# A rewritten exponential chain on VectorE, ten probability slots, five query sets

## The chip, the cores and the metric

The kernel runs on one core of a Trainium2 chip. The metric is the device time of one execution in microseconds (us); the median of five executions of the kernel before is 1861.48 us (1855.05 to 1868.85). The engines are TensorE (PE in the profile, with its weight loads as PEld), VectorE (DVE), ScalarE (ACT), GpSimd (POOL) and SyncE (SP). Each works through its own queue in order, and they wait for each other on semaphores.

## What is computed

Two layers, each an attention part and a mixer part, on 2048 positions of 512 features. Attention has 32 heads of 16 features that share one set of keys and values. Cut to what matters:

```
def _A_ref(x, wq, wk, wv, wo):               # H = 32, Dh = 16
    q = (x @ wq).reshape(B, S, H, Dh).transpose(0, 2, 1, 3)
    k = x @ wk
    v = x @ wv
    scores = einsum('bhqd,bkd->bhqk', q, k) * Dh ** (-0.5)
    p = softmax(scores, axis=-1)
    o = einsum('bhqk,bkd->bhqd', p, v)
    return o.transpose(0, 2, 1, 3).reshape(B, S, H * Dh) @ wo

def _B_ref(x, w_in, w_sp, b_sp, w_out):      # Fh = 896
    z = gelu(x @ w_in)
    z1, z2 = z[..., :Fh], layernorm(z[..., Fh:])
    g = einsum('ts,bsf->btf', w_sp, z2) + b_sp[None, :, None]
    return (z1 * g) @ w_out

x = x + _A_ref(layernorm(x), ...)
x = x + _B_ref(layernorm(x), ...)            # and both once more
```

The largest elementwise work is the exponential of the scores: 2 layers x 32 heads x 2048 x 2048 of them.

## The kernel before

**Blocks and units.** A group is a set of queries that fill 512 columns, for four partition groups of 32 (four heads at a time); 32 groups make a layer. For each of the 16 key tiles of 128, a group has one unit, and a unit has four blocks of 128 keys x 512 columns: 1024 units and 4096 blocks in all. For each block TensorE makes scores into PSUM (`_qk`, L1697), one engine turns them into probabilities in SBUF, and TensorE multiplies them with the values and adds up over the group's 16 units (PVStream, L1447). The value matrix has a column of ones, so the softmax denominator comes out with the sums, and the maximum is not subtracted. After a group VectorE evacuates (L815), the result is transposed and divided (L827, L839).

**Two engines for the exponential.** ScalarE takes scores from two rings of three and of two PSUM banks (FillStream, ExpStream, L1371) and writes to fifteen slots of `Pa`. VectorE takes single blocks from the remaining banks (DexStream) and writes to eight slots of `Pd`. It works on batches of two blocks: one instruction per block (L1554) turns the score into an integer, 65536 times the base-two logarithm of the result plus the exponent's bias; the low sixteen bits are then the fraction and the high ones the exponent. Six instructions over the whole batch follow (`chain`): u = fraction scaled to 0..1 (L1582), w = u - 1 (L1584), q = u w (L1588), u = B u + A (L1585), q = q u (L1591), and last the integer is scaled down, q is added, and the sum is written as a 16-bit integer whose bits are the bf16 probability (L1593).

**Order of the work.** A planner (`Sched`, at build time) simulates the engines with a list of costs (`d_sb`, `d_psum`, `d_act`) and delays (`LAT`) and commits operations greedily by readiness and priority; each engine's instructions are then written out in that order, with semaphore waits where an operation depends on another. Which block goes to which engine is decided there, too. When TensorE's next fill is committed, `DexStream.take` may give VectorE one block of a later unit, at least `LOOK` units ahead of the fill; it does so only if a bank is free, VectorE's backlog is under `BACKLOG`, fewer than two batches are open, and the slots of `Pd` that the batch will use have been read by their matmuls. It takes no block of the last `ENDX` units of a layer. `SoloStream` does the same between fills. VectorE has other work that the planner mixes in: query casts (L802), evacuations, layer norms and the mixer's sums (L1126, L1127).

**Query sets.** The queries of a group are projected into one of `NQS` sets in `qs` (`make_q`). `start_q` makes the first `NQS` of them; when the last score of a group has been made, `q_released` lets its set be made again for the group `NQS` further on.

**Shared scratch.** The tile `E` holds the chain's intermediates during attention, and the mixer's output weights and products at the end of a layer. [...]

Of the kernel before, what the change touches and what calls it, by code (L numbers as in the profile page):

```python
# [20 lines left out]
NF = 7  # L21
LN_EPS = 1e-5
SCALE = DH ** -0.5
# [338 lines left out]
    return progs  # L362


C_LOG2 = SCALE * 1.4426950408889634 * 65536.0
C_BIAS = 127.0 * 65536.0
C_A = 128.0 * 0.30449799
C_B = 128.0 * 0.07822817

LOOK = 6  # L370
NEAR = 4
URGENT = 1.0
BACKLOG = 3.0
# [1 line left out]
ENDX = 6  # L375
PR_LAST = 0.3
PR_SMALL = 0.6
NQS = 6
NPA = 15
NPD = 8  # L380
NWS = 16


# [4 lines left out]
def d_sb(n, rate):  # L388
    return n * rate + 0.066
# [10 lines left out]
def d_mm(n):  # L400
    return max(n / 2400.0 + 0.006, min(0.045 + n * 0.43e-3, 0.155))
# [19 lines left out]
class Kern:  # L421
    def __init__(self, nc, A_x, A_wq, A_wk, A_wv, A_wo, B_x, B_w_in, B_w_sp, B_b_sp, B_w_out, out):
# [15 lines left out]
        sc = self.sc = Sched([5, 7])  # L438
        self.nsb = 0
        sb = self.sb  # L440
# [295 lines left out]
    def layer_groups(self, layer):  # L736
        t0 = 0
        for ci, n in enumerate(self.chunks):
            nh = 512 // n
            for hg in range(0, 8, nh):  # L740
# [5 lines left out]
                q.index = g.index  # L746
                q.slot = q.index % NQS
                self.qsets.append(q)
# [34 lines left out]
    def make_q(self, q, war=()):  # L783
# [678 lines left out]
class DexStream:  # L1462
# [7 lines left out]
    def __init__(self, k):  # L1470
        self.k = k
        self.u = 0
        self.batch = []
        self.nb = 0
        self.cur = []
        self.open = []
        self.owner = [None] * NPD
        self.end = [None, None]
        self.last = []
        self.gate = None  # L1480

# [8 lines left out]
    def take(self, t, js):  # L1490

        k = self.k
        sc = k.sc
        if sc.bank_free() > t:
            return None
        base = 2 * (self.nb % (NPD // 2))
        if any(o.start is None and o.ready is not None and o.ready <= t for o in k.early_first):
            return None
        want = sum(o.first and o.prio < URGENT and o.ready <= t for o in sc.ready["pe"])
        if want and sum(not b.busy and not b.closed and b.free_at <= t for b in sc.banks) <= want:  # L1500
            return None
        if not self.batch:
            self.open = [o for o in self.open if o.start is None or o.end > t]
            if len(self.open) >= 2:
                return None
            backlog = sc.free["dve"] - t + sum(o.dur for o in sc.ready["dve"] if o.eng == "dve" and o.ready <= t)
            if backlog > BACKLOG:
                return None
            for i in range(2):
                w = self.owner[base + i]  # L1510
                if w is not None and w.pv is None:
                    return None
        fu = k.fill_s.u
        while fu < len(k.units) and all(b.kind is not None for b in k.units[fu].blocks):
            fu += 1
        if fu >= len(k.units):
            return None
        layer = k.units[fu].grp.layer
        u = max(self.u, fu + LOOK)
        while u < len(k.units):  # L1520
            un = k.units[u]
# [12 lines left out]
            u += 1  # L1534
        if u >= len(k.units):
            return None
        x = c[-1]
        x.kind = "D"
        self.u = u + 1
        if not self.batch:  # L1540
            self.ops = []
            self.s = self.nb % 2
            self.base = base
            self.war = [w.pv for w in self.owner[base:base + 2] if w is not None]
            self.nb += 1
        self.owner[self.base + len(self.batch)] = x.unit
        self.batch.append(x)
        return x

    def first_op(self, x, o, j):  # L1550
        k = self.k
        s = self.s
        i = len(self.batch) - 1
        c = k.sc.op("dve", lambda e: e.tensor_scalar(k.eI[:, s, 512 * i:512 * (i + 1)],  # L1554
                                                     k.b32(j.bank.idx)[:, 0:512], C_LOG2, C_BIAS, op0=ALU.mult, op1=ALU.add),
                    d_psum(512), [o, self.end[s]] + (self.gate or []), 2.0, job=j)
        c.unit = x.unit.index
        return c

    def after(self, c):  # L1560
        self.ops.append(c)
        if len(self.batch) == 2:
            self.flush()

    def flush(self):
# [4 lines left out]
    def chain(self, s):  # L1570
        k = self.k
        sc = k.sc
        nb = len(self.cur)
        n = 512 * nb
        I, u, w, q = k.eI[:, s, 0:n], k.eu[:, s, 0:n], k.ew[:, 0, 0:n], k.eq[:, s, 0:n]
        lo = I.bitcast(U16).rearrange("p (n two) -> p n two", two=2)[:, :, 0]
        base = self.base
        pr = 2.8

        def ts(out, a, m, b):  # L1580
            if b is None:
                return lambda e: e.tensor_scalar(out, a, m, None, op0=ALU.mult)  # L1582
            if m is None:
                return lambda e: e.tensor_scalar(out, a, b, None, op0=ALU.add)  # L1584
            return lambda e: e.tensor_scalar(out, a, m, b, op0=ALU.mult, op1=ALU.add)  # L1585
        o2 = sc.op("dve", ts(u, lo, 2.0 ** -16, None), d_sb(n, 0.521e-3), self.ops, pr)
        o3 = sc.op("dve", ts(w, u, None, -1.0), d_sb(n, 0.26e-3), [o2, getattr(self, "wfree", None)], pr)
        o4 = sc.op("dve", lambda e: e.tensor_tensor(q, u, w, ALU.mult), d_sb(n, 0.521e-3), [o3], pr)  # L1588
        self.wfree = o4
        o5 = sc.op("dve", ts(u, u, C_B, C_A), d_sb(n, 0.26e-3), [o4], pr)  # L1590
        o6 = sc.op("dve", lambda e: e.tensor_tensor(q, q, u, ALU.mult), d_sb(n, 0.521e-3), [o5], pr)  # L1591
        po = k.Pd[:, base:base + nb, :].rearrange("p k q -> p (k q)")
        o7 = sc.op("dve", lambda e: e.scalar_tensor_tensor(po.bitcast(U16), I, 2.0 ** -9, q, op0=ALU.mult, op1=ALU.add),  # L1593
                   d_sb(n, 1.042e-3), [o6] + self.war, pr)
        self.end[s] = o7
        for o in (o2, o3, o4, o5, o6, o7):
# [153 lines left out]
```

## Time and profile before

| | |
|---|---|
| median of five executions | 1861.48 us |
| the profiled execution's own time | 1867.65 us |
| its span | 1865.8 us |
| TensorE / VectorE / ScalarE busy | 1592.6 / 1736.4 / 1752.0 us |
| blocks turned into probabilities by ScalarE / VectorE | 3596 / 500 |
| VectorE batches | 251 |
| ScalarE's exp instructions | 1439 |
| mean granted TensorE clock | 0.98 |

A group line of the profile reads: source line, engine, operation, output <- inputs with their shapes, count; then busy time and mean duration in nanoseconds; then the idle time of the engine just before these instructions and what ended it. Rows of stretches give for each engine the busy time and, in brackets, the number of instructions. Durations on one engine can overlap, so a sum of durations may exceed the busy time.

### The profile page before, as it was taken

What the parts mean: (1) busy time and instruction counts of PE and PEld (TensorE: products, weight loads), DVE (VectorE), ACT (ScalarE), POOL (GpSimd) and SP (SyncE); (2) the same over time, 40 slices, a digit from 0 to 9 for tenths busy, and PEclk for the clock granted to TensorE, in tenths of its full rate; (3) what the DMA queues carried; (4) which work ended last, traced back from release to release, by engine and by line L of the source; (5) the groups of instructions that cost most, each with busy time, mean ns of one, the idle gap of its engine ahead of it and who ended that gap; (6) DMA issues with size and microseconds to landing.
All of it is one profiled execution on the core that took longest, in us unless ns stands there. A gap on an engine that the chain in (4) does not pass through costs nothing.

```text
span 1865.8 us, 30131 instructions
## 1 busy us (share of the span) xinstructions
PE 1592.6 (85%) x11779; PEld 475.5 (25%) x11868; DVE 1736.4 (93%) x3108; ACT 1752.0 (94%) x1577; POOL 48.0 (3%) x90
## 2 busy tenths in 40 slices
PE   8877888878889998898887878887788798989989
PEld 3222222112222222222431222221222222322334
DVE  8999999999989899987889999999999999999878
ACT  8999999999989999999569999999999999999983
POOL 2000000000000000000010000000000000000000
PEclk9999999899979999999999999999999999999999
DMA  9800001000010020111120000100000101011123
GB/s 261 208 1 1 10 9 30 1 1 18 7 40 23 24 46 21 46 57 55 48 52 1 1 1 10 37 1 1 1 15 10 40 24 32 15 43 35 60 63 110
DMA packets 122965, 68.04 MB, mean 36 GB/s; under 512 B 76996, under 2 KB 119240, under 8 KB 122824
## 3 DMA queue, kind: packets, MB, share of 16 engines
q1 hardware_dynamic: 121240, 65.95, 13.2%
q8 instruction: 94, 1.54, 0.3%
q14 instruction: 47, 0.39, 0.1%
q10 hardware_dynamic: 1584, 0.16, 0.1%
HBM read 30.97 MB, written 17.83 MB: 26 GB/s over the span
## 4 chain that ended last, share of the span: by engine, by line
ACT 40%; PE 22%; DVE 21%; issue 16%; DMA 1%; POOL 0%; SPq 0%; ACTq 0%; POOLq 0%; DVEq 0%
ACT Pa L1371 38%; PE ps_all L1697 6%; PE ps_all L1113 5%; PE ps_all L1447 4%; DVE E L1554 3%; DVE Pd L1593 3%; PE ps_all L1679 2%; DVE E L1588 2%; DVE E L1591 2%; DVE E L1582 2%; PE ps_all L936 1%; DVE st L631 1%; PE ps_all L1205 1%; DVE E L1585 1%; DVE E L1584 1%
## 5 line engine op out<-in xcount | busy, mean ns | idle before, releaser
L1371 ACT ACTIVATE Pa<-ps_all 128x1536 bf16<-128x1536 f32 (+1 forms) x1439 | 1636.8, 1365 | 31.5 <-PE ps_all L1697 29.4
L1697 PE MATMUL ps_all<-qs,kT 32*128 32x512 bf16 x4096 | 572.7, 390 | 194.4 <-ACT Pa L1371 176.9
L1554 DVE TENSOR_SCALAR E<-ps_all 128x512 int32<-128x512 f32 x500 | 341.2, 685 | 37.0 <-PE ps_all L1697 34.9
L1697 PEld LDWEIGHTS ps_all<-qs,kT 32*128 32x128 bf16 x4096 | 140.3, 91 | 750.0 <-ACT Pa L1371 688.1
L1447 PE MATMUL ps_all<-Pa,V 128*32 128x512 bf16 x3596 | 327.0, 391 | 0.0
L1593 DVE SCALAR_TENSOR_TENSOR Pd<-E 128x1024 uint16<-128x1024 int32 (+1 forms) x251 | 304.5, 1213 | 0.7
L1679 PE MATMUL ps_all<-zero 128*128 128x512 bf16 x780 | 260.6, 405 | 26.6 <-DVE E L1584 3.8
L1113 PE MATMUL ps_all<-wsT,z2n 128*128 128x512 bf16 x650 | 192.2, 391 | 13.3 <-issue 4.3
L1447 PE MATMUL ps_all<-Pd,V 128*32 128x512 bf16 x500 | 178.2, 392 | 0.0
L1588 DVE TENSOR_TENSOR E<-E 128x1024 f16<-128x1024 f16 (+1 forms) x251 | 171.6, 684 | 3.2
L1591 DVE TENSOR_TENSOR E<-E 128x1024 f16<-128x1024 f16 (+1 forms) x251 | 171.5, 683 | 2.4
L1582 DVE TENSOR_SCALAR E<-E 128x1024 f16<-128x1024 uint16 (+1 forms) x251 | 171.7, 684 | 1.6
L1585 DVE TENSOR_SCALAR E<-E 128x1024 f16<-128x1024 f16 (+1 forms) x251 | 105.1, 419 | 2.5
L1584 DVE TENSOR_SCALAR E<-E 128x1024 f16<-128x1024 f16 (+1 forms) x251 | 104.9, 418 | 2.4
L1679 PEld LDWEIGHTS ps_all<-zero 128*128 128x128 bf16 x780 | 61.1, 99 | 167.4 <-issue 91.6
L1447 PEld LDWEIGHTS ps_all<-Pa,V 128*32 128x32 bf16 x3596 | 64.7, 94 | 122.8 <-issue 116.7
L1126 DVE TENSOR_TENSOR gp<-ps_all,gp 128x512 f16<-128x512 f32 x112 | 75.3, 684 | 19.0 <-PE ps_all L1113 18.1
L1113 PEld LDWEIGHTS ps_all<-wsT,z2n 128*128 128x128 bf16 x714 | 54.5, 98 | 108.0 <-issue 64.7
L793 PE MATMUL ps_all<-xnTA,wq_pad 128*128 128x512 bf16 (+2 forms) x384 | 70.6, 310 | 1.3 <-DVE qs L802 0.7
L972 PE MATMUL ps_all<-xnTB,w_in_r 128*128 128x512 bf16 (+2 forms) x336 | 62.8, 311 | 4.0 <-DVE z1s L983 1.4
L936 PE MATMUL ps_all<-w_in_r,xnTB 128*128 128x448 bf16 x256 | 63.2, 356 | 1.3 <-DVE z2n L947 0.6
L1205 PE MATMUL ps_all<-E 128*128 128x512 bf16 x215 | 52.4, 380 | 4.7 <-DVE E L1190 1.8
(90 smaller groups left out, 1009.0 us busy)
## 6 DMA issues: line engine op xcount, KB each, us to landing
wsT_scratch<-gp SPq DMA_DIRECT2D x16, 512.0 KB, 3.9
wsT<-wsT_scratch SPq DMA_DIRECT2D x8, 1024.0 KB, 5.4
z1s<-z_scratch SPq DMA_DIRECT2D x16, 448.0 KB, 3.9
wsT<-wsT_scratch SPq DMA_DIRECT2D x8, 512.0 KB, 3.7
z_scratch<-z1s SPq DMA_DIRECT2D x4, 896.0 KB, 5.6
X<-in_A_x_dram SPq DMA_DIRECT2D x8, 256.0 KB, 5.3
out_dram<-X SPq DMA_DIRECT2D x16, 128.0 KB, 1.8
w_in_r<-in_B_w_in_dram SPq DMA_DIRECT2D x1, 1792.0 KB, 10.2
```

What stands on the lines that cost most here:

```text
L1113: ins = e.matmul(self.b32(b), self.z2n[:, s, f * 128:(f + 1) * 128], w_[:, s - s0, :] if s - s0 < na or not spare else wsp[:, s - s0 - na, :],
L1371: return e.activation(k.Pa[:, base:base + n, :], k.b32(b0, n).rearrange("p (k q) -> p k q", k=n), ACTF.Exp, scale=SCALE)
L1447: ins = e.matmul(k.b32(k.pvb)[32 * j:32 * j + 32, :], k.V[:, u.kt, 32 * j:32 * j + 32], b.slot, tile_position=(0, 32 * j), start=u.first, ...
L1554: c = k.sc.op("dve", lambda e: e.tensor_scalar(k.eI[:, s, 512 * i:512 * (i + 1)], k.b32(j.bank.idx)[:, 0:512], C_LOG2, C_BIAS, op0=ALU.mul ...
L1582: return lambda e: e.tensor_scalar(out, a, m, None, op0=ALU.mult)
L1584: return lambda e: e.tensor_scalar(out, a, b, None, op0=ALU.add)
L1585: return lambda e: e.tensor_scalar(out, a, m, b, op0=ALU.mult, op1=ALU.add)
L1588: o4 = sc.op("dve", lambda e: e.tensor_tensor(q, u, w, ALU.mult), d_sb(n, 0.521e-3), [o3], pr)
L1591: o6 = sc.op("dve", lambda e: e.tensor_tensor(q, q, u, ALU.mult), d_sb(n, 0.521e-3), [o5], pr)
L1593: o7 = sc.op("dve", lambda e: e.scalar_tensor_tensor(po.bitcast(U16), I, 2.0 ** -9, q, op0=ALU.mult, op1=ALU.add), d_sb(n, 1.042e-3), [o6] ...
L1679: return e.matmul(k.b32(k.pvb if b is None else b.idx), k.zero[:], k.zero[:, None, :].to_broadcast([P, 4, P]), start=b is not None, stop=b ...
L1697: return e.matmul(self.b32(bank), self.kT[32 * j:32 * j + 32, kt * 128:(kt + 1) * 128], self.qs[32 * j:32 * j + 32, g.q.slot, :], tile_pos ...
```

## The change

The score is no longer turned into an integer. L1554's successor writes fp32: 128 times the base-two logarithm plus 24576, a value in a range where the low sixteen bits of the fp32 mantissa are the fraction of the logarithm. From that fraction one instruction makes x, shifted and scaled (a multiply and an add). Then w = x x, w = w + C, w = w x, which is a cubic without its square term and so needs five instructions over the batch in place of six. The last instruction adds a constant and w to the fp32 score and writes 16 bits. The kinds of instruction, in order, are: scalar with two operations, product, scalar with one operation, product, closing.

The intermediates x and w have two buffers each (`NXW`); before, u and q had two and w one. `Pd` has ten slots in place of eight, VectorE's look-ahead is eight units in place of six, and there are five query sets in place of six. The batch is still two blocks (`NDB`). `E` becomes smaller.

```
-C_LOG2 = SCALE * 1.4426950408889634 * 65536.0
-C_BIAS = 127.0 * 65536.0
-C_A = 128.0 * 0.30449799
-C_B = 128.0 * 0.07822817
-
-LOOK = 6
+E_LOG2 = SCALE * 1.4426950408889634 * 128.0
+E_BIAS = 24576.0
+E_X = (128.0 * 0.07802455204644283) ** (1.0 / 3.0)
+E_A = 0.9657950762942451
+E_C = -6.696623932488385 * E_X * E_X
+E_D = 127.0 * 128.0 - E_BIAS + 128.0 * 0.43426538197757353
+NDB = 2
+NXW = 2
+
+LOOK = 8
...
-NQS = 6
+NQS = 5
 NPA = 15
-NPD = 8
+NPD = 10
...
-        E = sb([P, 9216], BF16, "E")
-        self.eI = E[:, 0:4096].bitcast(I32).rearrange("p (s n) -> p s n", s=2)
-        self.eu = E[:, 4096:6144].bitcast(FP16).rearrange("p (s n) -> p s n", s=2)
-        self.ew = E[:, 6144:7168].bitcast(FP16).rearrange("p (s n) -> p s n", s=1)
-        self.eq = E[:, 7168:9216].bitcast(FP16).rearrange("p (s n) -> p s n", s=2)
+        nb = 512 * NDB
+        E = sb([P, max((4 + 2 * NXW) * nb, NF * (D + 640))], BF16, "E")
+        self.ey = E[:, 0:4 * nb].bitcast(FP32).rearrange("p (s n) -> p s n", s=2)
+        xw = E[:, 4 * nb:(4 + 2 * NXW) * nb].bitcast(FP16).rearrange("p (two s n) -> p two s n", two=2, s=NXW)
+        self.ex, self.ew = xw[:, 0, :, :], xw[:, 1, :, :]
...
-        c = k.sc.op("dve", lambda e: e.tensor_scalar(k.eI[:, s, 512 * i:512 * (i + 1)],
-                                                     k.b32(j.bank.idx)[:, 0:512], C_LOG2, C_BIAS, op0=ALU.mult, op1=ALU.add),
+        c = k.sc.op("dve", lambda e: e.tensor_scalar(k.ey[:, s, 512 * i:512 * (i + 1)],
+                                                     k.b32(j.bank.idx)[:, 0:512], E_LOG2, E_BIAS, op0=ALU.mult, op1=ALU.add),
                     d_psum(512), [o, self.end[s]] + (self.gate or []), 2.0, job=j)
...
-        o2 = sc.op("dve", ts(u, lo, 2.0 ** -16, None), d_sb(n, 0.521e-3), self.ops, pr)
-        o3 = sc.op("dve", ts(w, u, None, -1.0), d_sb(n, 0.26e-3), [o2, getattr(self, "wfree", None)], pr)
-        o4 = sc.op("dve", lambda e: e.tensor_tensor(q, u, w, ALU.mult), d_sb(n, 0.521e-3), [o3], pr)
-        self.wfree = o4
-        o5 = sc.op("dve", ts(u, u, C_B, C_A), d_sb(n, 0.26e-3), [o4], pr)
-        o6 = sc.op("dve", lambda e: e.tensor_tensor(q, q, u, ALU.mult), d_sb(n, 0.521e-3), [o5], pr)
+        o2 = sc.op("dve", lambda e: e.tensor_scalar(x, lo, E_X * 2.0 ** -16, E_X * E_A, op0=ALU.mult, op1=ALU.add),
+                   d_sb(n, 0.521e-3), self.ops + [self.xfree[s % NXW]], pr)
+        o3 = sc.op("dve", lambda e: e.tensor_tensor(w, x, x, ALU.mult), d_sb(n, 0.521e-3), [o2, self.wfree[s % NXW]], pr)
+        o4 = sc.op("dve", lambda e: e.tensor_scalar(w, w, E_C, None, op0=ALU.add), d_sb(n, 0.26e-3), [o3], pr)
+        o5 = sc.op("dve", lambda e: e.tensor_tensor(w, w, x, ALU.mult), d_sb(n, 0.521e-3), [o4], pr)
         po = k.Pd[:, base:base + nb, :].rearrange("p k q -> p (k q)")
-        o7 = sc.op("dve", lambda e: e.scalar_tensor_tensor(po.bitcast(U16), I, 2.0 ** -9, q, op0=ALU.mult, op1=ALU.add),
-                   d_sb(n, 1.042e-3), [o6] + self.war, pr)
+        o7 = sc.op("dve", lambda e: e.scalar_tensor_tensor(po.bitcast(U16), y, E_D, w, op0=ALU.add, op1=ALU.add),
+                   d_sb(n, 1.042e-3), [o5] + self.war, pr)
+        self.xfree[s % NXW], self.wfree[s % NXW] = o5, o7
         self.end[s] = o7
```

More of the change, by code (lines that the diff above doesn't have):

```diff
@@ L1478, in __init__ @@
         self.end = [None, None]
+        self.xfree, self.wfree = [None] * NXW, [None] * NXW
         self.last = []
@@ L1495, in take @@
             return None
-        base = 2 * (self.nb % (NPD // 2))
+        base = NDB * (self.nb % (NPD // NDB))
         if any(o.start is None and o.ready is not None and o.ready <= t for o in k.early_first):
@@ L1508, in take @@
                 return None
-            for i in range(2):
+            for i in range(NDB):
                 w = self.owner[base + i]
@@ L1543, in take @@
             self.base = base
-            self.war = [w.pv for w in self.owner[base:base + 2] if w is not None]
+            self.war = [w.pv for w in self.owner[base:base + NDB] if w is not None]
             self.nb += 1
@@ L1561, in after @@
         self.ops.append(c)
-        if len(self.batch) == 2:
+        if len(self.batch) == NDB:
             self.flush()
@@ L1574, in chain @@
         n = 512 * nb
-        I, u, w, q = k.eI[:, s, 0:n], k.eu[:, s, 0:n], k.ew[:, 0, 0:n], k.eq[:, s, 0:n]
-        lo = I.bitcast(U16).rearrange("p (n two) -> p n two", two=2)[:, :, 0]
+        y, x, w = k.ey[:, s, 0:n], k.ex[:, s % NXW, 0:n], k.ew[:, s % NXW, 0:n]
+        lo = y.bitcast(U16).rearrange("p (n two) -> p n two", two=2)[:, :, 0]
         base = self.base
         pr = 2.8
[L1580 to L1585, printed above, removed]
-        o2 = sc.op("dve", ts(u, lo, 2.0 ** -16, None), d_sb(n, 0.521e-3), self.ops, pr)
-        o3 = sc.op("dve", ts(w, u, None, -1.0), d_sb(n, 0.26e-3), [o2, getattr(self, "wfree", None)], pr)
-        o4 = sc.op("dve", lambda e: e.tensor_tensor(q, u, w, ALU.mult), d_sb(n, 0.521e-3), [o3], pr)
-        self.wfree = o4
-        o5 = sc.op("dve", ts(u, u, C_B, C_A), d_sb(n, 0.26e-3), [o4], pr)
-        o6 = sc.op("dve", lambda e: e.tensor_tensor(q, q, u, ALU.mult), d_sb(n, 0.521e-3), [o5], pr)
+        o2 = sc.op("dve", lambda e: e.tensor_scalar(x, lo, E_X * 2.0 ** -16, E_X * E_A, op0=ALU.mult, op1=ALU.add),
[3 more added lines that the diff above has]
+        o5 = sc.op("dve", lambda e: e.tensor_tensor(w, w, x, ALU.mult), d_sb(n, 0.521e-3), [o4], pr)
         po = k.Pd[:, base:base + nb, :].rearrange("p k q -> p (k q)")
-        o7 = sc.op("dve", lambda e: e.scalar_tensor_tensor(po.bitcast(U16), I, 2.0 ** -9, q, op0=ALU.mult, op1=ALU.add),
-                   d_sb(n, 1.042e-3), [o6] + self.war, pr)
+        o7 = sc.op("dve", lambda e: e.scalar_tensor_tensor(po.bitcast(U16), y, E_D, w, op0=ALU.add, op1=ALU.add),
+                   d_sb(n, 1.042e-3), [o5] + self.war, pr)
+        self.xfree[s % NXW], self.wfree[s % NXW] = o5, o7
         self.end[s] = o7
-        for o in (o2, o3, o4, o5, o6, o7):
+        for o in (o2, o3, o4, o5, o7):
             o.unit = self.cur[0].unit.index
```

## The prediction

> **What bounds the kernel now.** I read the page first, then the engines by stretch of 100 us, then single lines by stretch, then VectorE's instructions in order of time, then who waits for whom. From the page (busy time; the costliest groups):
>
> ```profile
> span 1865.8 us, 30131 instructions
> ...
> PE 1592.6 (85%) x11779; PEld 475.5 (25%) x11868; DVE 1736.4 (93%) x3108; ACT 1752.0 (94%) x1577; POOL 48.0 (3%) x90
> ...
> L1371 ACT ACTIVATE Pa<-ps_all 128x1536 bf16<-128x1536 f32 (+1 forms) x1439 | 1636.8, 1365 | 31.5 <-PE ps_all L1697 29.4
> ...
> L1554 DVE TENSOR_SCALAR E<-ps_all 128x512 int32<-128x512 f32 x500 | 341.2, 685 | 37.0 <-PE ps_all L1697 34.9
> ...
> L1593 DVE SCALAR_TENSOR_TENSOR Pd<-E 128x1024 uint16<-128x1024 int32 (+1 forms) x251 | 304.5, 1213 | 0.7
> ...
> L1447 PE MATMUL ps_all<-Pd,V 128*32 128x512 bf16 x500 | 178.2, 392 | 0.0
> L1588 DVE TENSOR_TENSOR E<-E 128x1024 f16<-128x1024 f16 (+1 forms) x251 | 171.6, 684 | 3.2
> L1591 DVE TENSOR_TENSOR E<-E 128x1024 f16<-128x1024 f16 (+1 forms) x251 | 171.5, 683 | 2.4
> L1582 DVE TENSOR_SCALAR E<-E 128x1024 f16<-128x1024 uint16 (+1 forms) x251 | 171.7, 684 | 1.6
> L1585 DVE TENSOR_SCALAR E<-E 128x1024 f16<-128x1024 f16 (+1 forms) x251 | 105.1, 419 | 2.5
> L1584 DVE TENSOR_SCALAR E<-E 128x1024 f16<-128x1024 f16 (+1 forms) x251 | 104.9, 418 | 2.4
> ```
>
> ScalarE (ACT) and VectorE (DVE) are both nearly full: 4096 score blocks of 128x512 are shared out, 3596 to ScalarE's exp (L1371) and 500, in 251 batches of at most two, to VectorE's chain (L1554 to L1593). The chain is by far VectorE's largest work. By stretch (busy time of each engine):
>
> ```profile
> 100.00:200.00 100.00, 79.18 (x628) 20.35 (x624) 98.27 (x165) 100.00 (x90) 0.00 (x0) 1.00 0.00 1
> ...
> 600.00:700.00 100.00, 90.63 (x696) 28.20 (x706) 90.46 (x158) 97.48 (x87) 1.87 (x4) 1.00 0.13 32
> ...
> 1300.00:1400.00 100.00, 80.36 (x636) 21.33 (x636) 98.89 (x170) 99.92 (x89) 0.94 (x2) 1.00 0.04 8
> ```
>
> The columns are TensorE (PE), its weight loads, VectorE, ScalarE, GpSimd. From 100 to 500 and from 1000 to 1400 us there is hardly anything but attention: ScalarE 97 to 100%, VectorE 97 to 99%. There both limit together. From 500 to 800 and 1500 to 1700 the mixer's matmuls lie beside attention: ScalarE is still mostly at 93 to 99%, VectorE at 90 to 95%, TensorE at 87 to 91%. TensorE is not the limit in the first stretches: 26 of its 79 us in the first row are the filler matmuls of L1679.
>
> How VectorE's instructions follow each other decides what a removed one is worth (start, duration):
>
> ```profile
> 136.36 0.43 DVE L1584 TENSOR_SCALAR E<-E 128x1024 f16<-128x1024 f16 x1
> 136.82 0.69 DVE L1588 TENSOR_TENSOR E<-E 128x1024 f16<-128x1024 f16 x1
> ...
> 138.70 0.42 DVE L1585 TENSOR_SCALAR E<-E 128x1024 f16<-128x1024 f16 x1
> 139.03 0.69 DVE L1582 TENSOR_SCALAR E<-E 128x1024 f16<-128x1024 uint16 x1
> 139.64 0.69 DVE L1591 TENSOR_TENSOR E<-E 128x1024 f16<-128x1024 f16 x1
> 140.24 0.42 DVE L1584 TENSOR_SCALAR E<-E 128x1024 f16<-128x1024 f16 x1
> 140.57 1.22 DVE L1593 SCALAR_TENSOR_TENSOR Pd<-E 128x1024 uint16<-128x1024 int32 x1
> 141.71 0.69 DVE L1588 TENSOR_TENSOR E<-E 128x1024 f16<-128x1024 f16 x1
> ```
>
> Durations overlap: the next one starts 0.60 us after a 0.69 one, 1.14 after the 1.22 one, and after a 0.42 one 0.33 if it belongs to another batch, 0.46 if it needs that result.
>
> **The chain's arithmetic, part by part.** Before, a full batch takes two L1554 (0.60 each), L1582, L1588 and L1591 (0.60 each), L1584 and L1585 (0.33 to 0.46, say 0.40 each), L1593 (1.14): 3.00 + 0.80 + 1.14 = 4.94 us of VectorE. After it takes two score reads, one scale of the low halves, one square, one add, one product and the closing instruction: one of the short kind (0.40) less, 4.54 us. Priced one by one:
> - The score read writes fp32 in place of int32, with the same bytes. No row shows fp32 written from a 512-wide PSUM read; the reads that write bf16, fp16 and int32 all take 684 to 687 ns. Ends: 418 (the 512-wide SBUF product, L1187) and 686. I take 685, the common row.
> - The scale of the low halves now has a multiply and an add. L1585 (both) takes 419 and L1584 (one) 418, so the second operation is free; the stride of two stays, so 684 stays. [...]
> - The square reads one tile twice. It lies between the one-source row (419) and the two-source row (684); I take 684, since the instruction has two sources. [...]
> - The closing instruction reads fp32 in place of int32 and adds where it multiplied. Its 512-wide form takes 682 and the 1024-wide one 1217, so 535 ns for 512 columns or 1.04 ns a column. No row shows it with fp32; ends are 1217 and, if it should halve its rate, 1217 + 1067 (1024 more columns at 1.04). I take 1217: the four bytes are the same.
>
> So 251 x 0.40 = 100 us of VectorE come free (83 at 0.33, 115 at 0.46). [...]
>
> **What the freed time buys.** Freed VectorE time lies beside ScalarE's work; by itself it shortens nothing. It pays only as far as blocks move over. The order is written out by a greedy planner that gives VectorE a new batch when its backlog is small, so it will. ScalarE's price is 90 activations, 225 blocks, in 100 us of the first stretch: 0.444 us a block. VectorE's is 4.54 / 2 = 2.27. With x more blocks on VectorE both get shorter by T: T = 0.444 x and T = 100 - 2.27 x, so x = 37 and T = 16.4 us (18.9 for 115 freed us, 13.6 for 83). This holds where both are full: 141 of the 251 closing instructions start in 100 to 500 and 1000 to 1400 us, which gives 16.4 x 141/251 = 9.2. In the rest ScalarE is mostly full but VectorE has 5 to 10% idle already that the planner does not use, so I count half of the other 7.2: 3.6. Sum 12.8 us.
>
> **Slots, look-ahead, query sets.** These have one answer, near nothing. Units (16 key tiles a group, 4 blocks each) go by at 262 blocks in 100 us, 1.53 us each. A VectorE block is now read 8 units ahead, 12.2 us, in place of 9.2; two open chains take 2 x 4.94 = 9.9 before and 9.1 after, so the block is ready earlier relative to its use, not later. The slots are held two units longer, which the fifth pair of slots covers: one more batch of 4.54. The new waits (x and w per buffer, slot reuse after five batches) are on instructions two batches back on the same in-order queue, or on TensorE's use five batches back; behind them on VectorE stand the next batch and the evacuations L802, L815, L1126, for which TensorE waits. Their cover is that distance of two batches, 9 us; if it is gone, each such wait costs as much as rival 2 below. The best that more slots can do is to recover the 34.9 us VectorE idles before L1554: 34.9/2.71 x 0.444 = 5.7 us. Against: near a layer's end VectorE stops two units earlier, one block per layer, 2 x 0.444 = 0.9 us. Five query sets: a set is made again when its group's scores are done, four groups ahead of its use (4 x 16 x 1.53 = 98 us) instead of five (122). It takes 8 matmuls (0.38 each) and one cast (0.69), hidden by that lead; if it were not, a late set would stop scores for all. One of six is no longer made at the start, 3.7 us of work that comes back later. No DMA is issued differently, and SP's and POOL's queues are passed by nothing. Scratch moves cost nothing.
>
> Total: 12.8 - 0.9, about 12 us. The profiled execution took 1867.65 (span 1865.8 and 1.85 around it), 6.2 above the median; it would become 1855.7, and the median 1861.48 becomes 1849.5.
>
> **Rivals.**
> 1. The saved time stays idle: takes are tied to score fills and free banks, and VectorE waits 34.9 us for L1697 today. Then the count stays at 500, ScalarE keeps its 1637 us of exp, and the time is 1861 +- 4. For it: the 5 to 10% idle in the mixer stretches. Against: 98% in the pure ones, where idle is not left now. Chance 0.16.
> 2. Slower: TensorE's queue is in order, and probability times V (L1447 from Pd) stands in it ahead of later scores. If VectorE, loaded with some 268 batches, runs behind the planned order, that matmul waits, the next fills are late, and ScalarE idles. The idle before it is 0.0 today, and the look-ahead grows, which speaks against it; the planner knowing only its own costs speaks for it. At 0.1 us a batch it costs 27, so 1849.5 + 27 = 1876; it decides from 12/268 = 0.045 us a batch on, and is over 0.5% slower from 0.08. Chance 0.18, which also holds the worst ends of the square and the scale (0.53 us a batch, 133 freed us turned to a net loss of 33, about 5 us slower).
> 3. Twice the reach: idle before L1554 is recovered too, 16.4 + 5.7 = 22, 1839. Taken into the likeliest case as its far end.
>
> **How the numbers follow.** The likeliest case, blocks moving over, has 0.66; of it 0.60 beyond 0.5% (9.3 us, about what a measurement of this kernel can tell from no change) and 0.06 below. Same is 0.06 + 0.16 = 0.22, slower 0.18. The likeliest case alone spans 1838 to 1856. The whole range runs from 18.9 + 5.7 = 24.6 less, cut to 1838, to 1868, where about 0.1 of rival 2 is left out above.
>
> **What will show it.** Right: one short TENSOR_SCALAR line of the chain gone, the others at 685, 684, 684, 419, 684, 1217; some 525 score reads instead of 500; ScalarE's exp under 1630 us; VectorE still at 97% in the pure stretches; no idle at L1447 from Pd. Rival 1: still 500, VectorE near 92% there. Rival 2: idle before L1447 or more idle of L1371 on L1697. The prediction is wrong if a kept instruction changes its duration, or if the rewritten order lengthens the layer seams (860 to 1000 us, and 1800 on), which I hold unchanged.

## The result, and the profile after

The changed kernel takes 1852.05 us (median), the kernel before 1860.10 in the same comparison: ratio 0.9960, 95% interval 0.9950 to 0.9969, so about 7.4 us less. The profiled execution after took 1861.32 us (span 1859.2), 6.6 us of span less than the 1865.8 before. Like the one before it, it is a slow sample of its kernel, so its parts are compared with those of the profile before, not with the median. The granted clock of both is nearly the same, 0.982 and 0.980 in the mean.

The page after, the lines that answer to those shown before (line numbers have moved; L1559 is the score read, L1584 to L1590 the chain over the batch, L1375 ScalarE's exp, L1451 probabilities times V):

```profile
span 1859.2 us, 30024 instructions
...
PE 1591.4 (86%) x11797; PEld 477.6 (26%) x11881; DVE 1695.9 (91%) x2925; ACT 1741.4 (94%) x1566; POOL 50.5 (3%) x90
...
L1375 ACT ACTIVATE Pa<-ps_all 128x1536 bf16<-128x1536 f32 (+1 forms) x1432 | 1627.9, 1390 | 35.1 <-PE ps_all L1695 33.6
...
L1559 DVE TENSOR_SCALAR E<-ps_all 128x512 f32<-128x512 f32 x519 | 351.4, 684 | 43.5 <-PE ps_all L1695 41.5
...
L1590 DVE SCALAR_TENSOR_TENSOR Pd<-E 128x1024 uint16<-128x1024 f32 x260 | 315.9, 1215 | 1.8
...
L1451 PE MATMUL ps_all<-Pd,V 128*32 128x512 bf16 x519 | 181.4, 389 | 0.0
L1588 DVE TENSOR_TENSOR E<-E 128x1024 f16<-128x1024 f16 x260 | 177.8, 684 | 3.1
L1584 DVE TENSOR_SCALAR E<-E 128x1024 f16<-128x1024 uint16 x260 | 178.1, 686 | 2.5
L1586 DVE TENSOR_TENSOR E<-E 128x1024 f16<-128x1024 f16 x260 | 177.5, 683 | 2.6
L1587 DVE TENSOR_SCALAR E<-E 128x1024 f16<-128x1024 f16 x260 | 108.6, 418 | 1.8
```

Every instruction of the chain has the duration that the prediction took: score read 684, scale 686, square 683, add 418, product 684, closing 1215 ns. One short line is gone. The mean duration of ScalarE's exp reads 1390 ns in place of 1365, but its busy time per instruction is the same, 1627.9/1432 and 1636.8/1439, 1.137 us each: the durations overlap. VectorE has 519 blocks in place of 500, and still 0.0 us of idle before the matmuls that read `Pd`. VectorE is busy 40 us less (1695.9 against 1736.4): a part of the freed time was not used.

By stretch, after (columns as in the prediction):

```profile
100.00:200.00 100.00, 79.14 (x637) 20.13 (x629) 98.10 (x156) 100.00 (x90) 0.00 (x0) 1.00 0.00 1
...
700.00:800.00 100.00, 91.56 (x668) 28.59 (x672) 82.39 (x142) 98.09 (x84) 3.09 (x4) 1.00 0.17 54
```

In the attention-only stretches VectorE and ScalarE are as full as before. From 700 to 800 us, beside the mixer, it was before:

```profile
700.00:800.00 100.00, 88.37 (x624) 25.05 (x629) 95.32 (x169) 96.12 (x81) 2.78 (x4) 0.97 0.11 31
```

There VectorE fell from 95% to 82% while TensorE stands at 92%. Counting score reads by time says the same: in 100 to 500 and 1000 to 1400 us 275 of them start before and 296 after, in all the rest 225 before and 223 after.

To see where the 6.6 us came from I took the start of each group's evacuation (the cast to `oT`, L815 before, L819 after; 64 of them) from VectorE's order of time and cut the span at five of them. "Pure" is from the 2nd to the 18th and from the 33rd to the 50th (33 groups, attention nearly alone), "mixed" from the 18th to the 32nd and from the 50th to the 64th (28 groups), "seam" from layer 0's last evacuation to layer 1's first, "tail" from the last evacuation to the end of the span.

| us | first two | pure | mixed | seam | tail | span |
|---|---|---|---|---|---|---|
| before | 71.5 | 836.0 | 810.3 | 92.6 | 55.4 | 1865.8 |
| after | 76.0 | 824.4 | 804.6 | 95.9 | 58.3 | 1859.2 |
| difference | +4.5 | -11.6 | -5.7 | +3.3 | +2.9 | -6.6 |

The groups gained 17.3 us, and 10.7 were given back before the second group, between the layers and behind the last group.

Not all of these differences need belong to the change. In the traces TensorE's granted clock is either 1.00 or, for 3.4 us or a few times that, 0.50 (the half clock), and these falls lie elsewhere in each trace. From 60 to 80 us, before (where the fall comes at 73 us, behind the second evacuation):

```profile
60.00:80.00 20.00, 16.42 (x119) 4.07 (x119) 19.43 (x35) 18.86 (x17) 0.00 (x0) 0.91 1.16 269
```

and after:

```profile
60.00:80.00 20.00, 17.50 (x103) 3.76 (x102) 17.08 (x27) 16.80 (x16) 0.00 (x0) 0.74 1.09 275
```

The granted clock is the third number from the end. TensorE does 103 matmuls in place of 119, and ScalarE is busy 2 us less. Time at the half clock, before and after: none and 10.2 us in the first two groups, none and 10.2 in the seam, 37.5 and 17.1 in the pure groups, 37.5 and 30.7 in the mixed ones, none in either tail. So this pair alone shows the change's worth neither in the groups nor in the seam; the tail's +2.9 is free of the clock.

What lies in the tail: the mixer's spatial sums (L1113 before, L1117 after) that are still undone when attention ends. TensorE's busy time and count of them in the tail, before:

```profile
1810.40:1865.80 55.40, 13.07 (x55) 5.31 (x56) 1.00 0.31 92
```

and after:

```profile
1800.90:1859.20 58.30, 18.86 (x78) 7.34 (x78) 1.00 0.31 95
```

The attention ended 9.5 us earlier, but 78 matmuls of the sums were left instead of 55. In the seam it was the other way: 29 left after, 36 before. This suggested two theories besides the count of blocks (theory A), which the runs were to tell apart: that the order which the greedy planner happens to write decides as much as the count (theory B), and that the layers' ends belong to the spatial sums (theory D). Theory C gives the gain to slots, look-ahead and query sets.

### The profile page after: what moved, and what is told of

Read it like the earlier page. It is cut to its first block, busy times and chain, and to the rows that moved or that the text cites. A ratio compares the mean times of both kernels' runs of the same rounds, so it can differ in the third digit from the quotient of the medians.

```text
span 1859.2 us, 30024 instructions
## 1 busy us (share of the span) xinstructions
PE 1591.4 (86%) x11797; PEld 477.6 (26%) x11881; DVE 1695.9 (91%) x2925; ACT 1741.4 (94%) x1566; POOL 50.5 (3%) x90
## 3 DMA queue, kind: packets, MB, share of 16 engines
q1 hardware_dynamic: 121240, 65.95, 13.2%
## 4 chain that ended last, share of the span: by engine, by line
ACT 42%; PE 23%; DVE 17%; issue 17%; POOL 1%; DMA 0%; ACTq 0%; POOLq 0%
ACT Pa L1375 40%; PE ps_all L1695 6%; PE ps_all L1117 6%; PE ps_all L1451 4%; DVE E L1559 3%; DVE Pd L1590 2%; PE ps_all L1209 2%; PE ps_all L1677 1%; DVE E L1588 1%; DVE E L1586 1%; DVE st L635 1%; DVE E L1584 1%; DVE st L1031 1%; PE ps_all L940 1%; DVE gp L1130 1%
## 5 line engine op out<-in xcount | busy, mean ns | idle before, releaser
L1375 ACT ACTIVATE Pa<-ps_all 128x1536 bf16<-128x1536 f32 (+1 forms) x1432 | 1627.9, 1390 | 35.1 <-PE ps_all L1695 33.6
L1559 DVE TENSOR_SCALAR E<-ps_all 128x512 f32<-128x512 f32 x519 | 351.4, 684 | 43.5 <-PE ps_all L1695 41.5
L1451 PE MATMUL ps_all<-Pa,V 128*32 128x512 bf16 x3577 | 326.9, 390 | 0.1
L1590 DVE SCALAR_TENSOR_TENSOR Pd<-E 128x1024 uint16<-128x1024 f32 x260 | 315.9, 1215 | 1.8
L1117 PE MATMUL ps_all<-wsT,z2n 128*128 128x512 bf16 x656 | 190.1, 388 | 10.4 <-issue 4.3
L1451 PE MATMUL ps_all<-Pd,V 128*32 128x512 bf16 x519 | 181.4, 389 | 0.0
L1588 DVE TENSOR_TENSOR E<-E 128x1024 f16<-128x1024 f16 x260 | 177.8, 684 | 3.1
L1584 DVE TENSOR_SCALAR E<-E 128x1024 f16<-128x1024 uint16 x260 | 178.1, 686 | 2.5
L1586 DVE TENSOR_TENSOR E<-E 128x1024 f16<-128x1024 f16 x260 | 177.5, 683 | 2.6
L1587 DVE TENSOR_SCALAR E<-E 128x1024 f16<-128x1024 f16 x260 | 108.6, 418 | 1.8
L1451 PEld LDWEIGHTS ps_all<-Pa,V 128*32 128x32 bf16 x3577 | 65.2, 94 | 124.2 <-issue 121.2
L1117 PEld LDWEIGHTS ps_all<-wsT,z2n 128*128 128x128 bf16 x714 | 54.2, 98 | 103.0 <-issue 60.5
L1188 ACT ACTIVATE E<-ps_all 128x512 f16<-128x512 f32 (+1 forms) x51 | 24.6, 549 | 28.4 <-PE ps_all L1176 28.3
```

The lines of the kernel that those rows point to most:

```text
L1117: ins = e.matmul(self.b32(b), self.z2n[:, s, f * 128:(f + 1) * 128], w_[:, s - s0, :] if s - s0 < na or not spare else wsp[:, s - s0 - na, :],
L1375: return e.activation(k.Pa[:, base:base + n, :], k.b32(b0, n).rearrange("p (k q) -> p k q", k=n), ACTF.Exp, scale=SCALE)
L1451: ins = e.matmul(k.b32(k.pvb)[32 * j:32 * j + 32, :], k.V[:, u.kt, 32 * j:32 * j + 32], b.slot, tile_position=(0, 32 * j), start=u.first, ...
L1559: c = k.sc.op("dve", lambda e: e.tensor_scalar(k.ey[:, s, 512 * i:512 * (i + 1)], k.b32(j.bank.idx)[:, 0:512], E_LOG2, E_BIAS, op0=ALU.mul ...
L1584: o2 = sc.op("dve", lambda e: e.tensor_scalar(x, lo, E_X * 2.0 ** -16, E_X * E_A, op0=ALU.mult, op1=ALU.add), d_sb(n, 0.521e-3), self.ops ...
L1586: o3 = sc.op("dve", lambda e: e.tensor_tensor(w, x, x, ALU.mult), d_sb(n, 0.521e-3), [o2, self.wfree[s % NXW]], pr)
```

## The experiments

All ratios are to the kernel before, timed on the same chip together with the run. Every kernel's segments come from its own profile, cut as above. "Left" is the number of matmuls of the spatial sums in the tail and in the seam (the count may be low: the profile before has 840 weight loads at L1113 and 768 matmuls). The last column is the time that the profiled execution spent at the half clock, in all and in the pure groups.

| run | blocks | time, us | ratio [95%] | first two | pure | mixed | seam (left) | tail (left) | half clock, us (pure) |
|---|---|---|---|---|---|---|---|---|---|
| before | 500 | 1860.1 | 1 | 71.5 | 836.0 | 810.3 | 92.6 (36) | 55.4 (55) | 75.1 (37.5) |
| changed kernel | 519 | 1852.1 | 0.9960 [0.9950, 0.9969] | 76.0 | 824.4 | 804.6 | 95.9 (29) | 58.3 (78) | 68.3 (17.1) |
| e1 arithmetic alone | 523 | 1867.5 | 1.0046 [1.0034, 1.0058] | 71.9 | 828.3 | 800.9 | 103.7 (59) | 60.1 (73) | 61.4 (30.7) |
| e2 sixth instruction | 488 | 1865.1 | 1.0027 [1.0010, 1.0044] | 71.4 | 837.3 | 806.3 | 94.7 (28) | 54.2 (41) | 58.0 (34.1) |
| e3 old kernel, other order | 503 | 1870.7 | 1.0058 [1.0046, 1.0070] | 71.5 | 836.5 | 794.9 | 112.2 (80) | 54.2 (36) | 51.2 (41.0) |
| e4 new kernel, other order | 523 | 1856.7 | 0.9982 [0.9969, 0.9995] | 73.9 | 821.3 | 797.5 | 99.9 (61) | 59.4 (72) | 47.8 (10.2) |
| e5 four instructions | 560 | 1855.7 | 0.9983 [0.9965, 1.0000] | 71.5 | 822.7 | 793.0 | 111.5 (81) | 54.1 (47) | 64.8 (27.3) |
| e6 fewer sums, new | 517 | 1845.9 | 0.9939 [0.9919, 0.9960] | 73.0 | 827.9 | 801.6 | 91.8 (3) | 54.2 (32) | 54.6 (30.7) |
| e7 fewer sums, old | 496 | 1850.5 | 0.9970 [0.9953, 0.9987] | 71.5 | 833.4 | 808.7 | 90.9 (5) | 51.5 (6) | 58.0 (17.1) |
| e8 look-ahead 10, backlog 2 | 518 | 1834.4 | 0.9886 [0.9859, 0.9914] | 70.9 | 818.6 | 793.6 | 92.2 (29) | 53.2 (35) | 10.2 (0.0) |
| e9 as e8, sixth instruction | 493 | 1855.0 | 0.9974 [0.9959, 0.9989] | 72.9 | 830.4 | 804.0 | 92.8 (30) | 53.8 (28) | 27.3 (10.2) |
| e10 look-ahead 10 | 517 | 1852.4 | 0.9957 [0.9942, 0.9972] | 70.9 | 827.0 | 797.1 | 99.7 (57) | 53.7 (28) | 41.0 (23.9) |
| e11 backlog 2 | 519 | 1842.9 | 0.9910 [0.9894, 0.9925] | 73.0 | 825.6 | 800.6 | 92.3 (47) | 53.2 (30) | 44.4 (23.9) |
| e12 old kernel, third order | 503 | 1857.7 | 0.9988 [0.9976, 1.0001] | 71.5 | 833.1 | 799.5 | 92.8 (37) | 59.3 (74) | 47.8 (20.5) |

### The two halves of the change

The first run has the new arithmetic with the old sizes:

```
-LOOK = 8
+LOOK = 6
-NQS = 5
+NQS = 6
-NPD = 10
+NPD = 8
```

> The new arithmetic with the old eight slots, look-ahead of six and six query sets. The written-out order gives VectorE 523 blocks. Theory A (time follows the count of blocks, 0.444 us each): 23 fewer on ScalarE than the 500 of before, 10 us less, about 1850. Theory B (the greedy planner's order at the layer seam decides as much as the count): the groups' pace in the attention-only stretches is as with the whole change, but the seam, from the evacuation of layer 0's last group to that of layer 1's first (92.6 us before, 96.0 after), may be longer or shorter by up to 20 us, and the time moves by just that. Theory C (slots, look-ahead and sets bring the gain): no gain, 1860.

The second has the whole change but pays for the removed instruction again:

```
         o4 = sc.op("dve", lambda e: e.tensor_scalar(w, w, E_C, None, op0=ALU.add), d_sb(n, 0.26e-3), [o3], pr)
+        o4 = sc.op("dve", lambda e: e.tensor_scalar(w, w, 0.0, None, op0=ALU.add), d_sb(n, 0.26e-3), [o4], pr)
         o5 = sc.op("dve", lambda e: e.tensor_tensor(w, w, x, ALU.mult), d_sb(n, 0.521e-3), [o4], pr)
```

> The whole change, with one more short instruction over each batch (w plus zero, in place), so that a batch costs VectorE what it did before: slots, look-ahead and sets alone, in effect. The order gives VectorE 488 blocks. Theory A: 31 more on ScalarE than with the change, 13.8 us more than its 1852, about 1866. Theory C: still near 1852. Theory B: group pace back to that of before, seam open by 20 us either way.

Measured: 1867.5 and 1865.1 us, both slower than before. The arithmetic alone has 523 blocks on VectorE, 23 more than before, and its pure groups take 828.3 us, 7.7 less; its mixed groups are 9.4 faster as well (with 20.4 us less at the half clock there). Yet it loses 11.1 us in the seam and 4.7 in the tail, and its timed median is 8 us over the median of before in the same comparison (1859.7). So theory A falls as a theory of the total. The second run has the pure pace of before (837.3) and 488 blocks; A's 1866 is met. Theory C, that slots, look-ahead and query sets bring the gain without the cheaper chain, finds no support: with the old price they are 0.27% slower than before, and the pure pace is the old one. Neither half alone is faster. But each run also has an order of its own, and the next section shows that an order alone can move the time by 13 us; so these two runs do not show that the gain needs both halves.

### Nothing changed but the order

The planner's cost of a ScalarE instruction was moved by half a nanosecond to two. No instruction of any engine changes its kind; the greedy order does.

```
 def d_act(n):
-    return n * 0.8333e-3 + 0.051
+    return n * 0.8333e-3 + 0.0505
```

> The kernel before with nothing changed but the planner's cost of a ScalarE instruction, lower by half a nanosecond: same kinds of instructions, another order, 503 blocks to VectorE. Theory A: 1.3 us less, 1859. Theory B: same pace in the attention-only stretches, but the seam differs by many us, and the time with it, up to 20 us away from 1860.

The same line with 0.053 in the changed kernel:

> The changed kernel with nothing altered but the planner's cost of a ScalarE instruction, higher by two nanoseconds: another order, 523 blocks to VectorE. Theory A: 4 more blocks, 1850. Theory B: the pace of the changed kernel, the seam many us away from 96.0, and the time with it.

The same line with 0.050 in the kernel before:

> The kernel before, the planner's cost of a ScalarE instruction lower by a nanosecond; 503 blocks, as many as in the run with half a nanosecond, which took 1870.7. By the count: the same 1870, or 1860. By the order: a different time, and with a short seam it is near the changed kernel's 1852.

Measured: 1870.7, 1856.7 and 1857.7 us. The two orders of the old kernel have 503 blocks each and differ by 13 us: theory A cannot tell them apart. Their pure groups agree (836.5 and 833.1); the seam holds the difference, 112.2 against 92.8, with some given back in the tail. No half clock lies in either seam, and the timed executions of the two have like mean clocks (0.986 to 0.992 and 0.981 to 0.992), so this is not the clock. The spatial sums in the seam, in the kernel before:

```profile
888.51:981.13 92.62, 8.48 (x36) 3.34 (x35) 1.00 0.20 50
```

and in e3:

```profile
874.80:987.02 112.22, 19.82 (x80) 7.54 (x83) 1.00 0.18 45
```

and in e12:

```profile
875.85:968.64 92.79, 8.53 (x37) 3.33 (x35) 1.00 0.20 50
```

Theory B is shown: a change of cost that no engine ever sees moves the time by 13 us, more than the 7.4 of the change under study. Over all fourteen kernels seam and tail follow what is left of the sums: with up to 47 matmuls left, seams of 90.9 to 95.9 us, with 57 to 61 left 99.7 to 103.7, with 80 and 81 left 112.2 and 111.5; tails of 51.5 to 54.2 with up to 47 left, 55.4 with 55, 58.3 to 60.1 with 72 to 78.

### One instruction fewer still

```
-        o4 = sc.op("dve", lambda e: e.tensor_scalar(w, w, E_C, None, op0=ALU.add), d_sb(n, 0.26e-3), [o3], pr)
-        o5 = sc.op("dve", lambda e: e.tensor_tensor(w, w, x, ALU.mult), d_sb(n, 0.521e-3), [o4], pr)
+        o5 = sc.op("dve", lambda e: e.tensor_tensor(w, w, x, ALU.mult), d_sb(n, 0.521e-3), [o3], pr)
```

> The whole change with the add of the constant to the square (w + C) left out as well, so that the probabilities on VectorE are wrong but the batch is one short instruction cheaper still. The order gives VectorE 560 blocks. Theory A: 41 blocks more than the change, 18.2 us less, 1834. Theory B: groups in the attention-only stretches follow each other faster by 41/4096 or so (24.9 us becomes 24.6), but what lies at the layers' ends takes part of it back: over 1840.

Measured: 1855.7 us with 560 blocks. The page of e5:

```profile
L1559 DVE TENSOR_SCALAR E<-ps_all 128x512 f32<-128x512 f32 x560 | 379.7, 683 | 44.1 <-PE ps_all L1694 41.2
```

41 blocks more than the change and not faster: A's 1834 is missed by 22 us. The mixed groups are the fastest of all (793.0, 11.6 less than with the change), but pure gains only 1.7 (with 10.2 us more at the half clock), and the seam is 111.5 us with 81 matmuls left in it. Attention ended sooner, more of the sums were left behind it, and the seam took the gain back; e3, whose seam is as long without any such gain, says that the order alone could do this too. B's "over 1840" holds.

### Taking the sums away

```
-                seq = ([] if acc else [None]) + list(range(s0, s1))
+                seq = ([] if acc else [None]) + list(range(s0, s0 + 1 if early else s1))
```

> The changed kernel; in the mixer's third spatial pass two of its three key tiles are left out, 56 matmuls fewer per layer (512 columns, one about every 0.21 us, so 12 us of TensorE per layer); the evacuations stay. Theory D (TensorE's spatial sums, not the exponential, hold the layers' ends, and are what is left over when attention ends sooner): the 78 such matmuls behind the last group become about 22, the tail of 58 us shrinks by about 5 and the seam of 96 by a few, 1842 or less. Rival: the tail is set by the last tiles' own chain of steps, the left-over matmuls lie beside it: tail 58 as before, time within 2 us of 1852 apart from the order.

> The kernel before with the same 56 matmuls per layer left out. Theory D: only 55 such matmuls lay behind its last group, most of them gone now, so its tail of 55 us shrinks by less than that of the changed kernel, about 2 to 3, and the distance between old and new arithmetic grows from 8 to 12 us or more. Rival: no change in the tail, distance 8.

Measured: 1845.9 and 1850.5 us. In the changed kernel the tail went from 58.3 to 54.2 us and the seam from 95.9 to 91.8. The tail's sums in e6:

```profile
1794.20:1848.40 54.20, 7.56 (x32) 2.95 (x31) 1.00 0.31 94
```

In the kernel before the tail went from 55.4 to 51.5 and the seam from 92.6 to 90.9. (The changed kernel's seam has 10.2 us at the half clock, that of e6 3.4, the other two none; no tail has any.) With the same 56 matmuls a layer gone, both ends are shorter in both kernels, and the rival's 58 us tail did not come. So the sums hold a part of the ends, but a small one: with only 3 to 6 matmuls left the seams are still 90.9 and 91.8 us and the tail of the old kernel 51.5. What holds these is not shown. Theory D's 1842 was missed by 4 us. Its second half missed too: the distance between old and new did not grow from 8 to 12, it is 4.6 us (0.9970 against 0.9939, each known to some 0.2%, so 4.6 is not clearly less than 8). Seam and tail regained 8.2 us in the new kernel and 5.6 in the old, and the pure and mixed groups moved by up to 3.5 us each with what is again another order. What one left-over matmul costs also varies: 46 fewer in the tail were worth 4.1 us, or 0.09 us each, and 44 more in e3's seam went with 19.6 us, or 0.45 each, twice the 0.22 us that one takes in a row of them (25 in 5.56 us, from 1815.92 us on before). That the closing steps, which need the finished sums, queue behind them in the second case is argued and not shown.

### Look-ahead and backlog

```
-LOOK = 8
+LOOK = 10
...
-BACKLOG = 3.0
+BACKLOG = 2.0
```

> The changed kernel with a look-ahead of ten units and a backlog limit of 2 in place of 3; 518 blocks to VectorE, one fewer than the change. Theory A: 1852. Theory B: the order decides; chosen among many settings as one whose seam is short, so up to 15 us less.

The same with the sixth instruction of e2:

> The look-ahead of ten and the backlog limit of 2, with the extra short instruction over each batch, so that VectorE pays the old price; 493 blocks. If the arithmetic is worth its 0.28 us a group in the attention-only stretches wherever the order is good: groups there 25.2 us apart in place of 24.85, some 9 us, and with the blocks of the other stretches up to 11 (25 blocks at 0.444): 1843 to 1846, still faster than the kernel before. If the long look-ahead alone made the difference: 1834.

Only the first of the two edits, and only the second:

> The changed kernel with the look-ahead of ten alone, backlog limit 3 as in the change; 517 blocks. If a longer look-ahead is the cause of the gain over the change: 1834. If it was the order that came out with the pair of settings: anywhere from 1834 to 1860, by the seam, the tail and whether the granted clock falls after the first long Gelu.

> The changed kernel with the backlog limit of 2 alone, look-ahead eight; 519 blocks, the same count as the change. By the count: 1852. By the order: up to 20 us from it, with the seam, the tail and the clock after the first Gelu.

Measured: 1834.4, 1855.0, 1852.4 and 1842.9 us. e8 beats both kernels (0.9886 of before) with one block fewer than the change. Its profile, with pure 818.6, mixed 793.6 and short ends, flatters it: it is the fastest of its six executions, 1830.6 us at a mean clock of 0.997. Another of them, at 0.984, took 1844.7; executions of the changed kernel at 0.984 took 1852.1 to 1858.6. So e8 is faster at the same clock too, by less than its profile says. Look-ahead alone gives 1852.4, the same as the change, with a seam of 99.7; the backlog limit alone gives 1842.9 with exactly the change's 519 blocks. The latter is clear of the change (0.9910 and 0.9960, the intervals do not meet), but its pure groups are not (825.6 and 824.4). So neither setting has an effect of its own that was shown apart from its order; the pair was chosen among many for the short seam of its order. e9 says what the arithmetic is worth in that order, as far as an order can be kept: 0.9974 against 0.9886, 16 us by the ratios. The two profiles differ by 25 (pure 11.8, mixed 10.4, the ends 3.2), but e9's has 17 us more at the half clock. The 1843 to 1846 expected was missed by 9 us or more.

## Why the prediction was right or wrong

Forecast: 12 us less, median 1849.5, range 1838 to 1868. Measured: 0.9960, 7.4 us less, inside the range and in the direction forecast. It is under the 0.5% that the prediction took as the least that can be told from no change; that outcome had 0.22 where a larger gain had 0.60, and blocks moving over with so small a gain had only 0.06. At like mean clocks the distance is much the same, 5 to 7 us: executions at 0.988 to 0.990 have a median of 1855.7 us before and 1849.0 after, at 0.982 to 0.984 it is 1860.8 and 1855.6 (those before are from the comparisons with e1, e5 and e9).

**The chain's arithmetic** was right in every term: one short TENSOR_SCALAR gone, no duration off by more than 3 ns (the lines of the page above). The unknowns, the square that reads one tile twice and the closing instruction on fp32, came out near the values taken, 683 and 1215 ns; the end of 2284 ns did not occur. The closing instruction costs no more with fp32 (1215 ns) than with int32 (1213). The worst ends of the square and the scale, 0.53 us a batch in the chance of rival 2, are shown by no run: the square took 683 ns and the scale 686.

VectorE's starts again overlap. From the order of time after:

```profile
130.39 0.69 DVE L1586 TENSOR_TENSOR E<-E 128x1024 f16<-128x1024 f16 x1
131.12 0.43 DVE L1587 TENSOR_SCALAR E<-E 128x1024 f16<-128x1024 f16 x1
131.54 0.69 DVE L1559 TENSOR_SCALAR E<-ps_all 128x512 f32<-128x512 f32 x1
132.15 0.68 DVE L1588 TENSOR_TENSOR E<-E 128x1024 f16<-128x1024 f16 x1
```

The 0.43 us add takes 0.42 here, the 0.69 score read 0.61: 0.40 as the price of a short instruction stands.

**What the freed time buys, pure stretches.** Forecast 9.2 us (138 closing instructions start in these stretches, not 141, which would make it 9.0). The profile pair gives 11.6; over the six kernels with the old price per batch pure takes 830.4 to 837.3 us (mean 834.4), over the seven with the new price 818.6 to 828.3 (mean 824.7): 9.7 us, and the two ranges don't touch. Within each price the pure time follows the time at the half clock: with the new price 818.6 us with none, 821.3 with 10.2, 824.4 with 17.1, 825.6 and 827.0 with 23.9, 827.9 and 828.3 with 30.7. Two kernels of unlike price with the same time at the half clock are e9 and e4 (10.2 us): 830.4 and 821.3, or 9.1 apart; and e7 and the changed kernel (17.1): 833.4 and 824.4, or 9.0. So the arithmetic is worth about 9 us there, as forecast; it shows in every order that was tried, and some of the pair's 11.6 goes with the clock. Whether the falls of the clock lengthen the groups, or stalls of TensorE cause both, is not shown.

**The mixed stretches.** Half of 7.2, so 3.6 us, was a guess between ends. The profile pair gives 5.7, the means of the same kernels 803.9 and 799.4 or 4.5; but the ranges overlap (794.9 to 810.3 and 793.6 to 804.6), and the old price has more time at the half clock there, 25.6 us against 19.5 in the mean. So a gain there is not shown. The way it was to come did not occur: no block moved over outside the pure stretches (225 before and 223 after), where TensorE was at up to 92%; I had read VectorE's idle there as room. That 3.6 lies near 4.5 and 5.7 is luck.

**Where the prediction failed** is, besides the mixed stretches, its last sentence, "the layer seams (860 to 1000 us, and 1800 on), which I hold unchanged", together with the 0.9 us allowed for the ends. First groups, seam and tail took 10.7 us back, and by the prediction's own sign of being wrong it was wrong in this. Of the 10.7, the tail's 2.9 came with 78 matmuls of the sums left in place of 55 and no half clock in either. The first groups' 4.5 and the seam's 3.3 came with 10.2 us at the half clock each where the profile before has none; e8 and e10, with the same arithmetic and no half clock there, take 70.9 us for the first two. What holds is thus some 9 us won in the pure groups and 3 lost in the tail, 6 of the 7.4 measured. What the first groups, the mixed groups and the seam add is open.

The total landing inside the range is partly luck as well. Over the fourteen kernels first groups, seam and tail add up to 214 to 238 us, and the order alone moved the time of the old kernel by 13. The forecast of a change in a greedily ordered kernel needed a term for the order itself, some 10 us either way, and the range had it only by the rivals.

**Rivals.** The first, that the time stays idle, is wrong for the pure stretches (21 blocks more) and right for the count in the others. The second, a wait of TensorE on late `Pd`, did not occur: the idle before that matmul is 0.0 us. Its other sign did show a little, more idle of ScalarE's exp on scores (33.6 us, 29.4 before); why is open, e8 has 10.2 with the same arithmetic. The third's idle before the score read was not recovered, it grew from 34.9 to 41.5 us; its 1839 was passed only by e8 with other settings.

**Slots, look-ahead and query sets** were held near nothing. By themselves they were not tried one at a time; e1 with the old ones and the changed kernel differ by 0.86% in the ratios, not much more than the 0.70% between e3 and e12, which is order alone. Whether they have a worth of their own is open.

## What to carry to other kernels

Where a planner writes the order greedily, vary something that no engine sees (a cost constant) and time it before you believe a difference of half a per cent: here that alone moved the time by 13 us, and the change under study by 7. Judge an edit by the stretch in which it acts, cut at recurring events such as the evacuation of a group; the pure groups of kernels with the same price lay within 10 us where their totals spread over 33 (1834.4 to 1867.5). Read the granted clock of each stretch beside its time: one profile is one execution, and here two of the differences between the profiles before and after came with falls of the clock that the other profile did not have there. And ask what the faster part leaves behind: in the tail, more of another engine's work was waiting.

## What the runs showed of the hardware

TensorE's granted clock was 1.00 or 0.50 in these traces, and each fall to 0.50 lasted 3.4 us or a whole multiple of it: of the 143 that lie wholly inside the fourteen profiles, 99 lasted 3.4 us, 31 twice, 9 three times, 2 four times and 2 six times that. They came in the attention-only stretches too, and their number differs between executions of one and the same kernel: the mean clock of the changed kernel lay between 0.979 (1860.7 us) and 0.990 (1846.9 to 1849.4), that of e8 between 0.984 (1844.7) and 0.997 (1830.6).

The longest, six times 3.4 us, came in the profiles before and after, behind the first long Gelu in layer 0, in which ScalarE makes no probabilities (502.7 to 517.6 us before) and TensorE does little but filler matmuls (L1679, on zeros, 8.3 of its 12.8 us in the first row below). No run leaves these out, so what they do to the clock is not shown. Stretches of 20 us in the kernel before (the columns are as above):

```profile
500.00:520.00 20.00, 12.82 (x72) 3.91 (x69) 19.63 (x42) 19.94 (x11) 0.00 (x0) 1.00 0.14 47
520.00:540.00 20.00, 19.43 (x88) 3.77 (x89) 15.42 (x29) 15.28 (x13) 3.15 (x2) 0.52 0.14 46
```

and in e8:

```profile
500.00:520.00 20.00, 13.18 (x70) 3.58 (x69) 18.80 (x41) 19.97 (x11) 2.82 (x2) 1.00 0.28 92
520.00:540.00 20.00, 17.90 (x140) 5.47 (x135) 18.68 (x33) 18.75 (x17) 0.00 (x0) 1.00 0.00 1
```

In the second rows, TensorE does 88 matmuls in 20 us with the clock at 0.52 and 140 with it at 1.00, and ScalarE, which before waits 4.2 us there for scores, is busy 15.28 us in place of 18.75. In 520 to 540 us the clock was 0.52 to 0.66 in four profiles (before, after, e6, e7), whose groups 18 to 32 took 406.1 to 408.5 us, and 0.83 to 1.00 in the ten others, with 392.4 to 404.4. TensorE's busy time in the 20 us ahead of it is nearly the same in both (12.8 and 13.2 us), so that does not tell which execution loses the clock. From 500 to 520 us in the kernel before TensorE was never idle for more than 1.4 us at a time. What sets off a fall is not shown. One profile per kernel cannot tell whether the order decides it or the execution; that was not tried.
